# Holding back the first down-projection of each block, and tracking the residual in two column halves

## The chip, the cores and the metric

One core of one Trainium2 chip runs the whole program. The metric is the device time of one execution in microseconds (us); a kernel's figure is the median of its runs. A ratio is the mean time of one kernel's fast runs over the mean of the other's fast runs in the same rounds, so it is not quite the ratio of the medians; its 95% interval is in brackets.

## The reference, cut to what matters

Four layers run in turn on x of 2048 tokens x 576 columns: linear attention, bilinear unit, linear attention, bilinear unit. Each adds its result to x.

```python
def _B_ref(x, w_gate, w_up, w_down):          # F = 4608
    g = jnp.einsum("bsd,df->bsf", x, w_gate)
    u = jnp.einsum("bsd,df->bsf", x, w_up)
    h = g * u
    return jnp.einsum("bsf,fd->bsd", h, w_down)

x = x + _A_ref(_layernorm(x), A_wqkv, A_w_phi, A_wo)
x = x + _B_ref(_layernorm(x), B_w_gate, B_w_up, B_w_down)
# ... the same two lines once more
```

The change is in the bilinear unit.

## The kernel before

The kernel is written as coroutines, one for each piece of work. A scheduler, which runs when the kernel is built, asks each coroutine for its next group of instructions, estimates when that group could start, and takes the earliest. So every engine gets a **static order**. A tracker holds named keys (`("x", 5)` is row tile 5 of x) and places a semaphore wait wherever two instructions touch one key, and, for an accumulator bank in PSUM (`excl`), wherever two engines do.

The bilinear unit goes through 8 blocks of 256 tokens. A block has 36 rounds, one for each 128 columns of F. In a round TensorE does ten gate/up matmuls, ScalarE copies the gate half, VectorE multiplies (the product, `hT`), and TensorE does four down-projection matmuls, for the product of two rounds earlier (`LAG = 2`). These add up, over the block, in three banks: X and Y hold 512 columns of each half of the tokens, Z holds the remaining 64 columns of both. At the end of the block an epilogue of four VectorE adds moves the sums into x. There is only one set of X, Y, Z.

```python
        for i in range(total + LAG):
            if i < total:
                ...                                     # ten gate/up matmuls, copy, product
            if i >= LAG:
                b2, f2 = divmod(i - LAG, NF)            # NF = 36
                ...
                if f2 == 0 and b2 > 0:
                    yield ("wait", ("x2", L, b2 - 1))   # order: after the epilogue
                ...
                for sl in range(2):
                    bank = X if sl == 0 else Y
                    ...
                    ops.append(Op(d_pe(512), (... ps[:, bank, 0:512] ...), writes=[("acc", sl)], excl=[("pb", bank)]))
                    ops.append(Op(d_pe(64) + 6, (... ps[:, Z, 64 * sl:64 * sl + 64] ...), writes=[("accZ", sl)], excl=[("pb", Z)]))
                yield ("ops", "pe", ops)
                ...
                if f2 == NF - 1:
                    yield ("go", s.t_bepi(L, b2, on_block_done), 8, "bepi%d" % b2)
    ...
    def t_bepi(self, L, b, on_block_done):
        ...
        for sl in range(2):
            ...
            ops.append(Op(d_dve(512), (... tensor_tensor(xa, ps[:, bank, 0:512], xa, ALU.add)),
                          reads=[("acc", sl), ("x", st_)], writes=[("x", st_)], excl=[("pb", bank)]))
        for sl in range(2):
            ...
            ops.append(Op(d_dve(64), (... tensor_tensor(xb, ps[:, Z, 64 * sl:64 * sl + 64], xb, ALU.add)),
                          reads=[("accZ", sl), ("x", st_)], writes=[("x", st_)], excl=[("pb", Z)]))
```

While the first blocks of a bilinear unit run, the output half of the attention layer before it is still under way for later tokens. Its matmuls are mixed into the rounds of blocks 0 to 3 ("mixed stretch"). Blocks 4 to 7 are the "pure stretch".

Of the kernel before, what the change touches and what calls it, by code (L numbers as in the profile page):

```python
# [240 lines left out]
class Sched:  # L241
# [63 lines left out]
    def run(self):  # L305
        tr = self.tr
        while True:
# [50 lines left out]
            for th in self.threads:  # L358
                r = th.req
                if r[0] == "ops":  # L360
                    eng = r[1]
                    deps = []
                    for o in r[2]:
                        deps.extend(tr.deps_for(eng, o.reads, o.writes, o.excl))
                    est = max(self.free_at[eng], tr.ready_time(deps), th.t_ready)
                elif r[0] == "dma":
                    deps = tr.deps_for("sp", r[3], r[4], (), False)
                    est = max(self.free_at["sp"], tr.ready_time(deps), th.t_ready)
                else:
                    continue  # L370
                key = (est - self.bias.get(th.prio, 0.0), -th.prio)
                if best is None or key < best[0]:
                    best = (key, th, est)
            if best is None:
# [3 lines left out]
            _, th, est = best  # L378
# [42 lines left out]
CH = 3  # L421
# [3 lines left out]
def d_pe(n):  # L425
    return max(n, 64) / 2.4 + (7.0 if 288 <= n < 512 else 3.0)
# [18 lines left out]
class K:  # L445
    def __init__(self, nc, A_x, A_wqkv, A_w_phi, A_wo, B_w_gate, B_w_up, B_w_down, out, nlayers=4, dump=None):
        self.nc = nc
        self.A_x, self.A_wqkv, self.A_w_phi, self.A_wo = A_x, A_wqkv, A_w_phi, A_wo
        self.wg, self.wu, self.wd, self.out = B_w_gate, B_w_up, B_w_down, out
        self.nlayers = nlayers  # L450
        self.dump = dump
        self.nln0 = 3
        self.early = 2
        self.NPS, self.NSM, self.NVX, self.NET, self.NXP, self.NWD = 2, 4, 2, 3, 3, 3
        self.sbuf_check = True
        self.tr = Tracker()
        self.sc = Sched(self.tr)
        self.stack = ExitStack()
# [145 lines left out]
    def t_load(self):  # L604
# [10 lines left out]

        def xload(j):
            return grp("x%d" % j, [((lambda e: e.dma_start(s.x_sb[:, 4 * j:4 * j + 4, :], xv[:, 4 * j:4 * j + 4, :])),
                                    [("x", t) for t in range(4 * j, 4 * j + 4)], 128 * 4 * D * 2)], ("ld", "x", j))

        def rawload(which, kt):  # L620
            off = 0 if which == "q" else D
# [17 lines left out]
        for kt in range(5):  # L639
# [4 lines left out]
            ((lambda e: e.dma_start(s.Wvr[0:64, :], wqkv[512:576, 2 * D:2 * D + 324])), [("Wvr",)], 64 * 324 * 2),  # L644
            ((lambda e: e.dma_start(s.Wvr[64:128, 0:252], wqkv[512:576, 2 * D + 324:3 * D])), [("Wvr",)], 64 * 252 * 2),
        ], ("ld", "wv"))
        for j in range(1, 4):
            yield from xload(j)
        for kt in range(5):
            yield from rawload("q", kt)  # L650
        wov = s.A_wo[0:512, :].rearrange("(k p) n -> p k n", p=128)
        yield from grp("wo", [
            ((lambda e: e.dma_start(s.Wo[:], wov)), [("Wo",)], 512 * D * 2),
# [14 lines left out]
    def t_fuse(self, which):  # L668
# [2 lines left out]
        yield ("wait", "init")  # L671
        yield ("wait", "bdphi")
        if which == "q":
            yield ("wait", ("ain", 1, 1))
        yield ("go", s.t_fuse2(which), 6.6 if which == "q" else 8, "fuse2" + which)
        for kt in range(5):
            yield ("wait", ("ld", "raw", which, kt))
# [55 lines left out]
    def t_ln(self, b, sig):  # L733
# [6 lines left out]
        for j in range(2):  # L740
            for h in range(2):
                ops.append(Op(d_dve(288), (lambda e, j=j, h=h: e.bn_stats(st[:, sl[j], 6 * h:6 * h + 6], x_sb[:, ss[j], 288 * h:288 * h + 288])),
                              reads=[("x", ss[j])], writes=[("st", sl[j], h)]))
        yield ("ops", "dve", ops)
        ops = []
        for j in range(2):
# [15 lines left out]
        for j in range(2):  # L762
            ops.append(Op(800, (lambda e, j=j: e.tensor_scalar(  # L763
                xln[:, sl[j], 0:576], x_sb[:, ss[j], :], nm[:, sl[j]:sl[j] + 1], rstd[:, sl[j]:sl[j] + 1],
                ALU.add, ALU.mult)),
                reads=[("x", ss[j]), ("nmean", pair), ("rstd", pair), ("xlnpad",)], writes=[("xln", sl[j])]))
        yield ("ops", "pool", ops)
        for j in range(2):
            got = yield ("acq", ["pb", "pbx"])
# [107 lines left out]

    def t_ain(self, L, st_):
        s = self
        yield ("wait", ("w", "k"))  # L880
        ps_ = yield ("acq", "psb")
        sm = yield ("acq", "sm")
        yield ("go", s.t_v(L, st_), 6 + (NS - st_) / 100.0, "v%d_%d" % (L, st_))
        yield from s.softmax_front(st_, ps_, sm, s.Wk, s.Wkr, ("Wk",), ("Wkr",), ["pb", "pbx"])
        yield ("wait", ("v", L, st_))
        vxs = s.vx_of[(L, st_)]
# [33 lines left out]
    def t_aout(self, L, st_):  # L920
# [75 lines left out]
        for h in range(2):  # L996
# [3 lines left out]
            for k in range(5):  # L1000
# [3 lines left out]
                else:  # L1004
# [4 lines left out]
            yield ("ops", "pe", ops)  # L1009
            xs = s.x_sb[:, st_, 288 * h:288 * h + 288]  # L1010
            yield ("ops", "dve", [Op(d_dve(288), (lambda e, xs=xs, bank=bank: e.tensor_tensor(xs, s.ps[:, bank, 0:288], xs, ALU.add)),
                                     reads=[("pbd", bank), ("x", st_)], writes=[("x", st_)], excl=[("pb", bank)])])
            yield ("rel", got[0], got[1])
        yield ("rel", "et", et)
        yield ("sig", ("x1", L, st_))
# [16 lines left out]

    def t_bmain(self, L, on_block_done):
        s = self
        LAG = 2
        NG, NH = s.NG, s.NH
        ps, xT, Wg, Wu, Wr, gsb, hT = s.ps, s.xT, s.Wg, s.Wu, s.Wr, s.gsb, s.hT
        total = NB * NF
# [2 lines left out]
        yield ("wait", ("w", "q"))  # L1041
        yield ("wait", ("w", "k"))
        x0 = x1 = None
        X, Y, Z = s.ACC0, s.ACC0 + 1, s.ACC0 + 2
        for i in range(total + LAG):
            if i < total:
# [22 lines left out]
                if L == 1 and i < max(NG, NH):  # L1069
# [3 lines left out]
                yield ("ops", "dve", [Op(425, (lambda e, g=g, h=h, gub=gub: e.tensor_tensor(hT[:, h, :], ps[:, gub, 256:512], gsb[:, g, :], ALU.mult)),  # L1073
                                         reads=[("GUu", gub), ("gsb", g)], writes=[("hT", h)] + al, excl=[("pb", gub)])])
            if i >= LAG:
                b2, f2 = divmod(i - LAG, NF)
                h2 = (i - LAG) % NH
                c, fi = divmod(f2, CH)
                if f2 == 0 and b2 > 0:
                    yield ("wait", ("x2", L, b2 - 1))  # L1080
                if x0 is None:
                    gx = yield ("acqn", ["pbx"], 2)
                    x0, x1 = gx[0][1], gx[1][1]
                if fi == 0:
                    yield ("wait", ("wd", L, b2, c))
                slot = s.wd_slot[(L, b2, c)]
                ops = []
                for sl in range(2):
                    bank = X if sl == 0 else Y
                    lhsT = hT[:, h2, 128 * sl:128 * sl + 128]  # L1090
                    ops.append(Op(d_pe(512), (lambda e, lhsT=lhsT, bank=bank, slot=slot, fi=fi, f2=f2: e.matmul(  # L1091
                        ps[:, bank, 0:512], lhsT, s.wdr[:, slot, fi, 0:512], start=(f2 == 0), stop=(f2 == NF - 1))),
                        reads=[("hT", h2), ("wdr", slot)], writes=[("acc", sl)], excl=[("pb", bank)]))
                    ops.append(Op(d_pe(64) + 6, (lambda e, lhsT=lhsT, sl=sl, slot=slot, fi=fi, f2=f2: e.matmul(  # L1094
                        ps[:, Z, 64 * sl:64 * sl + 64], lhsT, s.wdr[:, slot, fi, 512:576],
                        start=(f2 == 0 and sl == 0), stop=(f2 == NF - 1), skip_group_check=True)),
                        reads=[("hT", h2), ("wdr", slot)], writes=[("accZ", sl)], excl=[("pb", Z)]))
                yield ("ops", "pe", ops)
                if fi == CH - 1:
                    yield ("rel", "wd", slot)  # L1100
                if f2 == NF - 1:
                    yield ("go", s.t_bepi(L, b2, on_block_done), 8, "bepi%d" % b2)
        yield ("wait", ("x2", L, NB - 1))
        yield ("rel", "pbx", x0)
        yield ("rel", "pbx", x1)
# [1 line left out]
    def t_bepi(self, L, b, on_block_done):  # L1107
        s = self
        ps, x_sb = s.ps, s.x_sb
        X, Y, Z = s.ACC0, s.ACC0 + 1, s.ACC0 + 2  # L1110
        ops = []
        for sl in range(2):
            st_ = 2 * b + sl
            bank = X if sl == 0 else Y
            xa = x_sb[:, st_, 0:512]
            ops.append(Op(d_dve(512), (lambda e, xa=xa, bank=bank: e.tensor_tensor(xa, ps[:, bank, 0:512], xa, ALU.add)),  # L1116
                          reads=[("acc", sl), ("x", st_)], writes=[("x", st_)], excl=[("pb", bank)]))
        for sl in range(2):
            st_ = 2 * b + sl
            xb = x_sb[:, st_, 512:576]  # L1120
            ops.append(Op(d_dve(64), (lambda e, xb=xb, sl=sl: e.tensor_tensor(xb, ps[:, Z, 64 * sl:64 * sl + 64], xb, ALU.add)),  # L1121
                          reads=[("accZ", sl), ("x", st_)], writes=[("x", st_)], excl=[("pb", Z)]))
        yield ("ops", "dve", ops)
        yield ("sig", ("x2", L, b))
        nxt = on_block_done(L, b)
        if nxt is not None:
            yield ("go", nxt, 6, "next%d_%d" % (L, b))

    def t_store(self, b):
        s = self  # L1130
        ov = s.out[0].rearrange("(t p) d -> p t d", p=128)
        yield ("dma", s.g_out, (lambda e: e.dma_start(ov[:, 2 * b:2 * b + 2, :], s.x_sb[:, 2 * b:2 * b + 2, :])),
               [("x", 2 * b), ("x", 2 * b + 1)], [("out", b)], 128 * 2 * D * 2, True)

    def t_layerA(self, L, first):
        s = self
# [47 lines left out]
    def build(self):  # L1184
        self.alloc()
        sc, tr, s = self.sc, self.tr, self
        self.g_out = tr.dma_group("out")
        sc.bias = {10: 300.0}
        sc.launch(self.t_init(), 9, "init")
        sc.launch(self.t_load(), 9, "load")  # L1190
        sc.launch(self.t_bdphi(), 9, "bdphi")
# [57 lines left out]
```

## Time and profile before

| | |
|---|---|
| time, median of the first 5 runs | 1257.26 us (1253.32 to 1259.26) |
| profiled span | 1254.8 us |
| attention input, layer 1 and layer 2 | about 0 to 130 us and 645 to 745 us |
| bilinear stretches | about 130 to 645 us and 745 to 1252 us |
| undisturbed round | 1.58 us |

The page of the kernel before: the span, the busy time of TensorE (PE) and its weight loads (PEld) with their shares of the span, the chain of work that ended last by engine and by line, and two groups of instructions (count, busy us, mean ns, idle before them and its releaser). L1058 and L1063 are the gate/up matmuls, L1091 and L1094 the down-projection of 512 and 64 columns.

```profile
span 1254.8 us, 25589 instructions
...
PE 1189.6 (95%) x10930; PEld 936.1 (75%) x11096; DVE 620.5 (49%) x1478; ACT 547.1 (44%) x1393; POOL 272.9 (22%) x268
...
PE 84%; DVE 5%; POOL 5%; ACT 4%; issue 1%; DMA 0%; SPq 0%; DVEq 0%
...
L1091 PE MATMUL ps<-wdr,hT 128*128 128x512 bf16 x986 | 318.8, 380 | 0.0
...
L1094 PE MATMUL ps<-wdr,hT 128*128 128x64 bf16 x1152 | 221.9, 193 | 14.8 <-DVE x_sb L1121 6.4
```

TensorE is the bound: 95% busy, 84% of the chain. The group of L1091 counts 986 matmuls where the group of L1094 has 1152; there are as many of one as of the other in the kernel, so 166 records are missing.

The view of waits of the same kernel (engine, tile, line, what it waited for: us in total, times, longest):

```profile
PEld ps L1094 <- DVE x_sb L1121: 6.4, 9, 0.8
PE ps L1094 <- DVE x_sb L1121: 6.4, 8, 0.8
```

TensorE waits 8 times for the last add of the epilogue (L1121). One such place in the timeline (start us, length us, engine, line, instruction; DVE is VectorE):

```profile
588.65 0.19 PE L1094 MATMUL ps<-wdr,hT 128*128 128x64 bf16 x1
...
588.68 0.60 PE L1058 MATMUL ps<-xT,Wg 128*128 128x256 bf16 x4
...
589.14 1.28 DVE L1116 TENSOR_TENSOR x_sb<-ps,x_sb 128x512 bf16<-128x512 f32 x2
...
589.66 0.27 PE L1063 MATMUL ps<-xT,Wr 128*128 128x256 bf16 x1
...
590.33 0.35 DVE L1121 TENSOR_TENSOR x_sb<-ps,x_sb 128x64 bf16<-128x64 f32 x2
...
590.74 0.20 PE L1094 MATMUL ps<-wdr,hT 128*128 128x64 bf16 x1 [0.80 <-DVE x_sb L1121]
...
590.77 0.38 PE L1091 MATMUL ps<-wdr,hT 128*128 128x512 bf16 x1
...
591.02 0.60 PE L1058 MATMUL ps<-xT,Wg 128*128 128x256 bf16 x4
```

The last matmul of the old block starts at 588.65. One gate/up group (588.68 to about 589.8) fills the time. VectorE begins the four adds at 589.14 (it had the product before them, from 588.80, to finish), and ends them at about 590.68. The 64-column matmul runs at 590.74, and the next gate/up group at 591.02. From 588.68 to 591.02 are 2.34 us, where an undisturbed round has 1.58: 0.76 us are lost. The round length is the safer measure here: the record of the 512-column matmul between is one of those missing, so "0.80" cannot be split into run and wait.

In the mixed stretch the same boundary loses nothing, because five attention matmuls (L799) lie in the gap:

```profile
818.58 0.60 PE L1058 MATMUL ps<-xT,Wg 128*128 128x256 bf16 x4
...
819.67 0.65 PE L799 MATMUL ps<-Wq,xT 128*128 128x288 bf16 x4
...
819.95 0.35 DVE L1121 TENSOR_TENSOR x_sb<-ps,x_sb 128x64 bf16<-128x64 f32 x2
...
820.28 0.38 PE L1091 MATMUL ps<-wdr,hT 128*128 128x512 bf16 x1
```

### The profile page before, as it was taken

Reading aid. Unit: us, or ns where it says so; the run is one execution under the profiler, and the core shown is the slowest. Engines: PE = TensorE matmul, PEld = TensorE weight load, DVE = VectorE, ACT = ScalarE, POOL = GpSimd, SP = SyncE. Lnnn points to the kernel's source line nnn. Section 1 sums busy time; section 2 is a strip of 40 time slices with the busy share of each in tenths; the row PEclk is TensorE's granted clock in tenths of the full one; section 3 lists DMA queues with packets and bytes.
Section 4 is the critical chain, followed back from the end, with each engine's and each line's share of the span. In section 5 each row is a group of like instructions: output and inputs, shape, how many; then the busy total and the mean of one; then the engine's idle time right before and its main releaser. Section 6 shows DMA issues by size and latency. Waiting matters only on the chain.

```text
span 1254.8 us, 25589 instructions
## 1 busy us (share of the span) xinstructions
PE 1189.6 (95%) x10930; PEld 936.1 (75%) x11096; DVE 620.5 (49%) x1478; ACT 547.1 (44%) x1393; POOL 272.9 (22%) x268
## 2 busy tenths in 40 slices
PE   6796999999999999999999889999999999999998
PEld 4574788788777777777767668777778777777776
DVE  6898646555553323323259975455545332323232
ACT  7887545345453222222248765444444322222222
POOL 4796212112120000000029842112112000000000
PEclk9998999999999999999999899999999999999999
DMA  9700122232222233333320002222323232333332
GB/s 312 231 2 1 29 79 80 72 87 72 77 82 86 86 99 87 97 89 87 98 72 2 1 1 72 83 84 76 91 72 96 72 109 86 109 88 108 90 105 67
DMA packets 85832, 104.61 MB, mean 83 GB/s; under 512 B 4374, under 2 KB 84566, under 8 KB 84566
## 3 DMA queue, kind: packets, MB, share of 16 engines
q1 hardware_dynamic: 85718, 102.96, 27.5%
q8 instruction: 87, 1.43, 0.4%
q14 instruction: 27, 0.22, 0.1%
HBM read 100.59 MB, written 2.36 MB: 82 GB/s over the span
## 4 chain that ended last, share of the span: by engine, by line
PE 84%; DVE 5%; POOL 5%; ACT 4%; issue 1%; DMA 0%; SPq 0%; DVEq 0%
PE ps L1058 25%; PE ps L1063 25%; PE ps L1091 17%; PE ps L1094 5%; PE ps L799 4%; PE ps L1007 3%; POOL dd L860 3%; PE ps L934 2%; POOL dd L824 1%; PE ps L953 1%; DVE ss L846 1%; PE ps L774 1%; DVE x_sb L1116 1%; PE ps L986 1%; DVE dd L832 1%
## 5 line engine op out<-in xcount | busy, mean ns | idle before, releaser
L1073 DVE TENSOR_TENSOR hT<-ps,gsb 128x256 bf16<-128x256 f32 x576 | 244.2, 424 | 580.4 <-ACT gsb L1071 578.8
L1071 ACT CAST gsb<-ps 128x256 bf16<-128x256 f32 x576 | 214.5, 372 | 626.2 <-PE ps L1063 588.3
L1058 PE MATMUL ps<-xT,Wg 128*128 128x256 bf16 x2304 | 347.3, 273 | 0.0
L1063 PE MATMUL ps<-xT,Wu 128*128 128x256 bf16 x2304 | 346.1, 273 | 0.0
L1091 PE MATMUL ps<-wdr,hT 128*128 128x512 bf16 x986 | 318.8, 380 | 0.0
L1058 PEld LDWEIGHTS ps<-xT,Wg 128*128 128x128 bf16 x2304 | 186.4, 98 | 82.1
L1063 PEld LDWEIGHTS ps<-xT,Wu 128*128 128x128 bf16 x2304 | 225.7, 98 | 26.3
L1094 PE MATMUL ps<-wdr,hT 128*128 128x64 bf16 x1152 | 221.9, 193 | 14.8 <-DVE x_sb L1121 6.4
L860 POOL TENSOR_TENSOR dd<-dd,rr 128x576 bf16<-128x576 bf16 x128 | 146.3, 1164 | 120.1 <-ACT rr L854 120.0
L1091 PEld LDWEIGHTS ps<-wdr,hT 128*128 128x128 bf16 x1152 | 112.5, 98 | 75.1 <-DVE x_sb L1116 1.7
L1058 PE MATMUL ps<-xT,Wr 128*128 128x256 bf16 x576 | 157.3, 273 | 0.0
L1063 PE MATMUL ps<-xT,Wr 128*128 128x256 bf16 x576 | 157.1, 273 | 0.0
L763 POOL TENSOR_SCALAR xln<-x_sb,nmean,rstd 128x576 bf16<-128x576 bf16 x64 | 52.1, 825 | 364.4 <-ACT rstd L758 364.4
L824 POOL TENSOR_TENSOR dd<-psb,mxmn 128x576 bf16<-128x576 bf16 x64 | 74.5, 1164 | 237.8 <-DVE mxmn L814 237.7
L1094 PEld LDWEIGHTS ps<-wdr,hT 128*128 128x128 bf16 x1152 | 112.3, 98 | 12.5 <-DVE x_sb L1121 6.4
L846 DVE TENSOR_REDUCE ss<-dd 128x64 f32<-128x1152 bf16 x64 | 86.4, 1351 | 22.4 <-ACT dd L841 22.1
L1058 PEld LDWEIGHTS ps<-xT,Wr 128*128 128x128 bf16 x576 | 56.5, 98 | 6.6
L1063 PEld LDWEIGHTS ps<-xT,Wr 128*128 128x128 bf16 x576 | 56.4, 98 | 6.6
L811 ACT CAST psb<-ps 128x288 bf16<-128x288 f32 x128 | 48.0, 401 | 17.8 <-PE ps L799 15.8
L937 ACT COPY eT<-ps 108x768 bf16<-108x768 bf16 x64 | 50.9, 799 | 8.3 <-PE ps L953 4.9
L819 DVE TENSOR_REDUCE mxmn<-ps 128x16 f32<-128x288 f32 x128 | 52.0, 448 | 0.0
L832 DVE TENSOR_TENSOR dd<-ps,mxmn 128x288 bf16<-128x288 f32 x128 | 51.8, 448 | 0.0
(85 smaller groups left out, 1142.6 us busy)
## 6 DMA issues: line engine op xcount, KB each, us to landing
wdr<-in_B_w_down_dram SPq DMA_DIRECT2D x192, 432.0 KB, 3.4
Wg<-in_B_w_gate_dram SPq DMA_DIRECT2D x4, 1152.0 KB, 13.0
Wu<-in_B_w_up_dram SPq DMA_DIRECT2D x4, 1152.0 KB, 28.5
x_sb<-in_A_x_dram SPq DMA_DIRECT2D x4, 576.0 KB, 6.2
out_dram<-x_sb SPq DMA_DIRECT2D x8, 288.0 KB, 3.4
Wraw<-in_A_wqkv_dram SPq DMA_DIRECT2D x8, 144.0 KB, 4.8
Wv<-in_A_wqkv_dram SPq DMA_DIRECT2D x1, 576.0 KB, 4.0
Wo<-in_A_wo_dram SPq DMA_DIRECT2D x1, 576.0 KB, 6.3
```

The source lines that it names most:

```text
L763: ops.append(Op(800, (lambda e, j=j: e.tensor_scalar(xln[:, sl[j], 0:576], x_sb[:, ss[j], :], nm[:, sl[j]:sl[j] + 1], rstd[:, sl[j]:sl[j] ...
L819: ops.append(Op(370, (lambda e, h=h, pv=pv: e.tensor_reduce(mxmn[:, pz, 1, 16 * h:16 * h + 16], pv, AX.X, ALU.min)), reads=[("pbd", bank)] ...
L824: yield ("ops", "pool", [Op(1170, (lambda e: e.tensor_tensor(d1, p3, mxb, ALU.subtract)), reads=[("psb", pz, 0), ("psb", pz, 1), ("mx", pz ...
L832: ops.append(Op(370, (lambda e, d2h=d2h, pv=pv, mnbh=mnbh: e.tensor_tensor(d2h, pv, mnbh, ALU.subtract)), reads=[("pbd", bank), ("mn", pz, ...
L846: Op(1320, (lambda e: e.tensor_reduce(ss[:, sm, :].rearrange("p (b g) -> p b g", b=2), e4, AX.X, ALU.add)), reads=s.ddk(sm, 0) + s.ddk(sm, ...
L860: yield ("ops", "pool", [Op(1150, (lambda e, ev=ev, rb=rb: e.tensor_tensor(ev, ev, rb, ALU.mult)), reads=s.ddk(sm, br) + [("rr", sm), ("dd ...
L1058: ops.append(Op(d_pe(256), (lambda e, lhsT=lhsT, rhs=rhs, k=k, gub=gub: e.matmul(ps[:, gub, 0:256], lhsT, rhs, start=(k == 0), stop=(k == ...
L1063: ops.append(Op(d_pe(256), (lambda e, lhsT=lhsT, rhs=rhs, k=k, gub=gub: e.matmul(ps[:, gub, 256:512], lhsT, rhs, start=(k == 0), stop=(k = ...
L1071: yield ("ops", "act", [Op(372, (lambda e, g=g, gub=gub: e.copy(gsb[:, g, :], ps[:, gub, 0:256])), reads=[("GUg", gub)], writes=[("gsb", g ...
L1073: yield ("ops", "dve", [Op(425, (lambda e, g=g, h=h, gub=gub: e.tensor_tensor(hT[:, h, :], ps[:, gub, 256:512], gsb[:, g, :], ALU.mult)), ...
L1091: ops.append(Op(d_pe(512), (lambda e, lhsT=lhsT, bank=bank, slot=slot, fi=fi, f2=f2: e.matmul(ps[:, bank, 0:512], lhsT, s.wdr[:, slot, fi, ...
L1094: ops.append(Op(d_pe(64) + 6, (lambda e, lhsT=lhsT, sl=sl, slot=slot, fi=fi, f2=f2: e.matmul(ps[:, Z, 64 * sl:64 * sl + 64], lhsT, s.wdr[: ...
```

## The change

The intent is to give the epilogue more time: at a block boundary the first down-projection of the new block is kept back until one more gate/up group has been issued, and then two down-projections go out together. So that the two 64-column adds can each follow their 512-column add without waiting for it to complete, the key of a row tile of x is split in two halves of columns. The diff, cut to its core:

```diff
+        pend = []
         for i in range(total + LAG):
             ...
             if i >= LAG:
+                pend.append(i - LAG)
                 b2, f2 = divmod(i - LAG, NF)
-                ... (the down-projection of round i - LAG)
+                if f2 == 0 and b2 > 0 and i + 1 < total:
+                    continue
+                for j in pend:
+                    ... (the down-projection of round j)
+                pend = []
@@ t_bepi
-                          reads=[("acc", sl), ("x", st_)], writes=[("x", st_)], excl=[("pb", bank)]))
-        for sl in range(2):
-            st_ = 2 * b + sl
+                          reads=[("acc", sl), ("x", st_, 0)], writes=[("x", st_, 0)], excl=[("pb", bank)]))
             xb = x_sb[:, st_, 512:576]
             ...
-                          reads=[("accZ", sl), ("x", st_)], writes=[("x", st_)], excl=[("pb", Z)]))
+                          reads=[("accZ", sl), ("x", st_, 1)], writes=[("x", st_, 1)], excl=[("pb", Z)]))
```

All other users of x name both halves. The diff also turns some constants into attributes with the same values (`lag`, `bias`, and flags that are off), and the scheduler looks up its bias by the whole part of a priority.

More of the change, by code (lines that the diff above doesn't have):

```diff
@@ L370, in run @@
                     continue
-                key = (est - self.bias.get(th.prio, 0.0), -th.prio)
+                key = (est - self.bias.get(int(th.prio), 0.0), -th.prio)
                 if best is None or key < best[0]:
@@ L455, in __init__ @@
         self.sbuf_check = True
+        self.lag = 2
+        self.bias = {10: 300.0}
+        self.qfuse_after = ("ain", 1, 1)
+        self.rawq_early = False
+        self.v_early = False
         self.tr = Tracker()
@@ L617, in xload @@
             return grp("x%d" % j, [((lambda e: e.dma_start(s.x_sb[:, 4 * j:4 * j + 4, :], xv[:, 4 * j:4 * j + 4, :])),
-                                    [("x", t) for t in range(4 * j, 4 * j + 4)], 128 * 4 * D * 2)], ("ld", "x", j))
+                                    [("x", t, c_) for t in range(4 * j, 4 * j + 4) for c_ in range(2)], 128 * 4 * D * 2)], ("ld", "x", j))
         def rawload(which, kt):
@@ L646, in t_load @@
         ], ("ld", "wv"))
+        if s.rawq_early:
+            for kt in range(5):
+                yield from rawload("q", kt)
         for j in range(1, 4):
             yield from xload(j)
-        for kt in range(5):
-            yield from rawload("q", kt)
+        if not s.rawq_early:
+            for kt in range(5):
+                yield from rawload("q", kt)
         wov = s.A_wo[0:512, :].rearrange("(k p) n -> p k n", p=128)
@@ L673, in t_fuse @@
         if which == "q":
-            yield ("wait", ("ain", 1, 1))
+            yield ("wait", s.qfuse_after)
         yield ("go", s.t_fuse2(which), 6.6 if which == "q" else 8, "fuse2" + which)
@@ L742, in t_ln @@
                 ops.append(Op(d_dve(288), (lambda e, j=j, h=h: e.bn_stats(st[:, sl[j], 6 * h:6 * h + 6], x_sb[:, ss[j], 288 * h:288 * h + 288])),
-                              reads=[("x", ss[j])], writes=[("st", sl[j], h)]))
+                              reads=[("x", ss[j], 0), ("x", ss[j], 1)], writes=[("st", sl[j], h)]))
         yield ("ops", "dve", ops)
@@ L765, in t_ln @@
                 ALU.add, ALU.mult)),
-                reads=[("x", ss[j]), ("nmean", pair), ("rstd", pair), ("xlnpad",)], writes=[("xln", sl[j])]))
+                reads=[("x", ss[j], 0), ("x", ss[j], 1), ("nmean", pair), ("rstd", pair), ("xlnpad",)], writes=[("xln", sl[j])]))
         yield ("ops", "pool", ops)
@@ L879, in t_ain @@
         s = self
+        if s.v_early:
+            yield ("go", s.t_v(L, st_), 6 + (NS - st_) / 100.0, "v%d_%d" % (L, st_))
         yield ("wait", ("w", "k"))
@@ L882, in t_ain @@
         sm = yield ("acq", "sm")
-        yield ("go", s.t_v(L, st_), 6 + (NS - st_) / 100.0, "v%d_%d" % (L, st_))
+        if not s.v_early:
+            yield ("go", s.t_v(L, st_), 6 + (NS - st_) / 100.0, "v%d_%d" % (L, st_))
         yield from s.softmax_front(st_, ps_, sm, s.Wk, s.Wkr, ("Wk",), ("Wkr",), ["pb", "pbx"])
@@ L1011, in t_aout @@
             yield ("ops", "dve", [Op(d_dve(288), (lambda e, xs=xs, bank=bank: e.tensor_tensor(xs, s.ps[:, bank, 0:288], xs, ALU.add)),
-                                     reads=[("pbd", bank), ("x", st_)], writes=[("x", st_)], excl=[("pb", bank)])])
+                                     reads=[("pbd", bank), ("x", st_, 0), ("x", st_, 1)], writes=[("x", st_, 0), ("x", st_, 1)], excl=[("pb", bank)])])
             yield ("rel", got[0], got[1])
@@ L1034, in t_bmain @@
         s = self
-        LAG = 2
+        LAG = s.lag
         NG, NH = s.NG, s.NH
@@ L1075, in t_bmain @@
             if i >= LAG:
+                pend.append(i - LAG)
                 b2, f2 = divmod(i - LAG, NF)
-                h2 = (i - LAG) % NH
-                c, fi = divmod(f2, CH)
-                if f2 == 0 and b2 > 0:
-                    yield ("wait", ("x2", L, b2 - 1))
-                if x0 is None:
-                    gx = yield ("acqn", ["pbx"], 2)
-                    x0, x1 = gx[0][1], gx[1][1]
-                if fi == 0:
-                    yield ("wait", ("wd", L, b2, c))
-                slot = s.wd_slot[(L, b2, c)]
@@ L1087, in t_bmain @@
-                ops = []
-                for sl in range(2):
-                    bank = X if sl == 0 else Y
-                    lhsT = hT[:, h2, 128 * sl:128 * sl + 128]
-                    ops.append(Op(d_pe(512), (lambda e, lhsT=lhsT, bank=bank, slot=slot, fi=fi, f2=f2: e.matmul(
-                        ps[:, bank, 0:512], lhsT, s.wdr[:, slot, fi, 0:512], start=(f2 == 0), stop=(f2 == NF - 1))),
-                        reads=[("hT", h2), ("wdr", slot)], writes=[("acc", sl)], excl=[("pb", bank)]))
-                    ops.append(Op(d_pe(64) + 6, (lambda e, lhsT=lhsT, sl=sl, slot=slot, fi=fi, f2=f2: e.matmul(
-                        ps[:, Z, 64 * sl:64 * sl + 64], lhsT, s.wdr[:, slot, fi, 512:576],
-                        start=(f2 == 0 and sl == 0), stop=(f2 == NF - 1), skip_group_check=True)),
-                        reads=[("hT", h2), ("wdr", slot)], writes=[("accZ", sl)], excl=[("pb", Z)]))
@@ L1098, in t_bmain @@
-                yield ("ops", "pe", ops)
-                if fi == CH - 1:
-                    yield ("rel", "wd", slot)
-                if f2 == NF - 1:
-                    yield ("go", s.t_bepi(L, b2, on_block_done), 8, "bepi%d" % b2)
+                if f2 == 0 and b2 > 0 and i + 1 < total:
+                    continue
+                for j in pend:
+                    b2, f2 = divmod(j, NF)
+                    h2 = j % NH
+                    c, fi = divmod(f2, CH)
+                    if f2 == 0 and b2 > 0:
+                        yield ("wait", ("x2", L, b2 - 1))
+                    if x0 is None:
+                        gx = yield ("acqn", ["pbx"], 2)
+                        x0, x1 = gx[0][1], gx[1][1]
+                    if fi == 0:
+                        yield ("wait", ("wd", L, b2, c))
+                    slot = s.wd_slot[(L, b2, c)]
+                    ops = []
+                    for sl in range(2):
+                        bank = X if sl == 0 else Y
+                        lhsT = hT[:, h2, 128 * sl:128 * sl + 128]
+                        ops.append(Op(d_pe(512), (lambda e, lhsT=lhsT, bank=bank, slot=slot, fi=fi, f2=f2: e.matmul(
+                            ps[:, bank, 0:512], lhsT, s.wdr[:, slot, fi, 0:512], start=(f2 == 0), stop=(f2 == NF - 1))),
+                            reads=[("hT", h2), ("wdr", slot)], writes=[("acc", sl)], excl=[("pb", bank)]))
+                        ops.append(Op(d_pe(64) + 6, (lambda e, lhsT=lhsT, sl=sl, slot=slot, fi=fi, f2=f2: e.matmul(
+                            ps[:, Z, 64 * sl:64 * sl + 64], lhsT, s.wdr[:, slot, fi, 512:576],
+                            start=(f2 == 0 and sl == 0), stop=(f2 == NF - 1), skip_group_check=True)),
+                            reads=[("hT", h2), ("wdr", slot)], writes=[("accZ", sl)], excl=[("pb", Z)]))
+                    yield ("ops", "pe", ops)
+                    if fi == CH - 1:
+                        yield ("rel", "wd", slot)
+                    if f2 == NF - 1:
+                        yield ("go", s.t_bepi(L, b2, on_block_done), 8, "bepi%d" % b2)
@@ L1116, in t_bepi @@
             ops.append(Op(d_dve(512), (lambda e, xa=xa, bank=bank: e.tensor_tensor(xa, ps[:, bank, 0:512], xa, ALU.add)),
-                          reads=[("acc", sl), ("x", st_)], writes=[("x", st_)], excl=[("pb", bank)]))
-        for sl in range(2):
-            st_ = 2 * b + sl
+                          reads=[("acc", sl), ("x", st_, 0)], writes=[("x", st_, 0)], excl=[("pb", bank)]))
             xb = x_sb[:, st_, 512:576]
             ops.append(Op(d_dve(64), (lambda e, xb=xb, sl=sl: e.tensor_tensor(xb, ps[:, Z, 64 * sl:64 * sl + 64], xb, ALU.add)),
-                          reads=[("accZ", sl), ("x", st_)], writes=[("x", st_)], excl=[("pb", Z)]))
+                          reads=[("accZ", sl), ("x", st_, 1)], writes=[("x", st_, 1)], excl=[("pb", Z)]))
         yield ("ops", "dve", ops)
@@ L1132, in t_store @@
         yield ("dma", s.g_out, (lambda e: e.dma_start(ov[:, 2 * b:2 * b + 2, :], s.x_sb[:, 2 * b:2 * b + 2, :])),
-               [("x", 2 * b), ("x", 2 * b + 1)], [("out", b)], 128 * 2 * D * 2, True)
+               [("x", 2 * b, 0), ("x", 2 * b, 1), ("x", 2 * b + 1, 0), ("x", 2 * b + 1, 1)], [("out", b)], 128 * 2 * D * 2, True)
     def t_layerA(self, L, first):
@@ L1187, in build @@
         self.g_out = tr.dma_group("out")
-        sc.bias = {10: 300.0}
+        sc.bias = dict(self.bias)
         sc.launch(self.t_init(), 9, "init")
```

## The prediction

> **What bounds the kernel.** TensorE: the page gives it 1189.6 us busy of a 1254.8 us span (95%), and the chain of work that ended last is 84% TensorE. Two stretches (about 0 to 130 us and 645 to 745 us, attention input) are held by VectorE and GpSimd; the change does not touch those. In the two bilinear stretches one round (ten gate/up matmuls, then four down-projection matmuls) repeats every 1.58 us in the timeline (501.95 to 503.53), back to back.
>
> **The target.** At the end of each of 8 blocks per layer, four VectorE adds fold the accumulators into x. The first down-projection of the next block writes the same three banks, so it waits. In the timeline at 588.7 us: the old block's last down-projection ends about 588.8; the adds start at 589.14, after the product of the round before, and end about 590.68 (two of 681 ns, two of 215 ns, overlapping: 1.55 us); TensorE has only one gate/up group (1.09 us) to fill with, and its 64-column matmul starts at 590.74. That round took 2.34 us (588.68 to 591.02): 0.76 us too long. The Trainium skill, "PSUM — Partial Sum Buffer", section "Engine vs sequencer instructions", says that matmuls start and complete in program order and that VectorE's queue is strict FIFO. The trace agrees: the next gate/up group does not pass the blocked matmul.
>
> The view of waits lists this wait 8 times, 6.4 us in all. They are the boundaries at 414, 472, 530, 589, 1022, 1080, 1138 and 1195 us; the same eight show in the chain as VectorE adds of 1.28 us. The other six (209, 279, 349, 819, 889, 959 us) already have attention-output projections or transposes in the gap and lose at most 0.1 us.
>
> **What the change does.** It holds back a block's first down-projection by one round, so two gate/up groups (2.17 us) stand before it, then issues two together. No matmul, byte or VectorE operation is added or removed. TensorE then reaches the accumulators about 590.9, after the adds' release at 590.74: the wait goes, with a margin near 0.15 us. The ring of four hT buffers just suffices; the product of the held-back round must finish before its gate/up bank is written again: about 592.9 against 593.4, even when the four normalization statistics (1.53 us) go before it. Splitting the residual's key lets each 64-column add stand behind its 512-column add without waiting for it to complete; the four still take about 1.55 us. The other changed lines keep their old values.
>
> **Sum.** 8 x 0.76 = 6.1 us, all on the critical path as TensorE is the bound there. Against it: the static order in the mixed stretches is recomputed and may shift a microsecond either way. Expected 1257.3 - 6.1 = 1251.2 us (0.5%). Range 1246.5 to 1255.5, since runs of before alone spread 1253.3 to 1259.3. Chances: faster by over 2% 0.02, within 2% 0.97, slower 0.01.
>
> **What would show it.** Right: the down-projection's waits on the x adds (6.4 us) fall under 1 us; blocks in the pure stretch take 57.5 us instead of 58.25 in layer 1 (414.37 to 472.63) and 56.9 instead of 57.7 in layer 2; TensorE busy stays 1189 to 1190 us; the eight adds leave the chain; attention input phases keep their length. Wrong: a remaining wait of some tenths per boundary (margin too thin), a new TensorE wait on VectorE's product two rounds later, or a changed length in the mixed or attention phases from reordering. A gain well over 8 us would mean that the six covered boundaries also lost time, or that the reordering helped.

## The result, and the profile after

| | before | after |
|---|---|---|
| median | 1258.08 us (16 runs) | 1252.06 us (9 runs) |
| ratio | | 0.9955 [0.9943, 0.9967] |
| profiled span | 1254.8 us | 1252.0 us |

The result is 0.45% less time, and clear of noise. The page after; here L1109 and L1112 are the down-projection, L1071 and L1076 the gate/up matmuls, L1135 and L1138 the adds:

```profile
span 1252.0 us, 25573 instructions
...
PE 1192.3 (95%) x10930; PEld 938.3 (75%) x11096; DVE 619.6 (49%) x1478; ACT 547.1 (44%) x1393; POOL 272.9 (22%) x268
...
L1109 PE MATMUL ps<-wdr,hT 128*128 128x512 bf16 x986 | 316.9, 380 | 0.4 <-DVE x_sb L1135 0.4
...
L1112 PE MATMUL ps<-wdr,hT 128*128 128x64 bf16 x1152 | 221.9, 193 | 9.4 <-DVE x_sb L1138 0.5
```

The groups of the down-projection now show next to no idle time that the adds ended. The view of waits of TensorE from 745 us on has what is left; from 210.8 to 643 us there is none:

```profile
PE ps L1112 <- DVE x_sb L1138: 0.5, 1, 0.5
PE ps L1109 <- DVE x_sb L1135: 0.4, 1, 0.4
```

A pure boundary after the change, in the timeline:

```profile
530.79 0.19 PE L1112 MATMUL ps<-wdr,hT 128*128 128x64 bf16 x1
...
530.82 0.60 PE L1071 MATMUL ps<-xT,Wg 128*128 128x256 bf16 x4
...
531.27 0.68 DVE L1135 TENSOR_TENSOR x_sb<-ps,x_sb 128x512 bf16<-128x512 f32 x1
...
531.87 0.21 DVE L1138 TENSOR_TENSOR x_sb<-ps,x_sb 128x64 bf16<-128x64 f32 x1
531.91 0.60 PE L1071 MATMUL ps<-xT,Wg 128*128 128x256 bf16 x4
...
532.60 0.21 DVE L1138 TENSOR_TENSOR x_sb<-ps,x_sb 128x64 bf16<-128x64 f32 x1
...
532.89 0.27 PE L1076 MATMUL ps<-xT,Wr 128*128 128x256 bf16 x1
...
533.22 0.19 PE L1112 MATMUL ps<-wdr,hT 128*128 128x64 bf16 x1
```

Two gate/up groups (530.82 and 531.91) now lie between the two blocks. The adds end at about 532.81; the 64-column matmul comes at 533.22 with no wait before it. (The 512-column matmul before it has no record; by its width it starts 0.22 us earlier.) One whole block of the pure stretch, from its first add to the next block's, in the view of windows (us, then busy us and count of PE, PEld, DVE, ACT, POOL, then the granted clock, DMA share and GB/s), before and after:

```profile
472.63:530.88 58.25, 57.03 (x508) 44.78 (x515) 18.29 (x47) 15.65 (x43) 1.63 (x2) 1.00 0.32 92
```

```profile
473.78:531.27 57.49, 57.02 (x508) 44.88 (x515) 18.18 (x47) 15.55 (x43) 1.63 (x2) 1.00 0.32 94
```

TensorE is busy for the same 57.0 us and the block is 0.76 us shorter. (508 matmul records stand here against 515 weight loads. In after_again, the changed kernel profiled once more with no record missing, TensorE is busy for 57.50 of the 57.50 us of this block.) The page "TensorE: Matmul & The Clock Gate" of the Trainium skill (section "Wait — 56ns, not 53.3ns?") gives a warm matmul of N columns N / 2.4 GHz + about 2.5 ns from start to start. By this estimate the matmuls of this block, counted from the static order, make 57.50 us, which is what the trace has after the change: 57.49. With these matmuls at this rate TensorE has nothing left to gain there. (An undisturbed round has 3712 columns in 14 matmuls: 1.58 us by this sum and by the trace.)

**An account of all rounds.** The same sum can be set against every round: take the time between the first gate matmuls of two neighbouring rounds, and subtract what the matmuls between them (known from the static order) take at full speed. What remains is an estimate of the time that TensorE lost in that round; missing records do no harm. Losses by block, in us, from the traces:

```
                 layer 1, blocks 0..7                      layer 2, blocks 0..7
before           4.11 .03 .03 .17 .76 .76 .76 .76          2.47 .03  .03  .02 .76 .76 .76 .76
after            4.07 .18 .02 .17 .00 .00 .00 .00          2.44 .35 1.59  .02 .00 .00 .00 .00
```

So the change gains 8 x 0.76 = 6.1 us, and gives back 0.15 us in layer 1 and 1.9 us in layer 2. (What block 0 loses is the passage from the attention stretch; it varies from run to run with the clock, as the last section shows, and the change does not reach it.) The largest piece given back, 1.25 us, is at the boundary near 890 us:

```profile
887.97 0.19 PE L1112 MATMUL ps<-wdr,hT 128*128 128x64 bf16 x1
...
888.14 0.75 DVE L823 TENSOR_REDUCE mxmn<-psb 128x32 f32<-128x576 bf16 x1 [0.22 <-ACT psb L820]
...
888.81 0.81 DVE L828 TENSOR_REDUCE mxmn<-ps 128x16 f32<-128x288 f32 x2
...
890.04 0.68 DVE L1135 TENSOR_TENSOR x_sb<-ps,x_sb 128x512 bf16<-128x512 f32 x1
890.07 0.27 PE L1076 MATMUL ps<-xT,Wr 128*128 128x256 bf16 x1
...
890.77 0.39 PE L1109 MATMUL ps<-wdr,hT 128*128 128x512 bf16 x1 [0.43 <-DVE x_sb L1135]
...
891.64 0.20 PE L1112 MATMUL ps<-wdr,hT 128*128 128x64 bf16 x1 [0.47 <-DVE x_sb L1138]
```

The last matmul of the old block starts at 887.97, but VectorE first has three reductions of the attention output to do (888.14 and 888.81) and then the product (at 889.70), so the adds begin only at 890.04 instead of some 0.3 us after the block's end. Even two gate/up groups do not cover that. In the kernel before, attention matmuls lay in this gap and the reductions came after the adds. The smaller pieces are not at boundaries: in the two rounds that lose 0.32 us (at 826.67 and 896.18) five transposes of the attention output (L998) start at 828.07 and 897.58, just after the VectorE multiplication that makes their input (L987) ends (828.02 and 897.53).

Two profiles are no measure of a gain of this size: the spans differ by 2.8 us, the medians by 6. The first epilogue, up to which both kernels have one and the same TensorE order, came at 209.05 us in one and at 210.80 us in the other.

### The profile page after: what moved, and what is told of

The parts are those of the page before. It is cut to its first block, busy times and chain, and to the rows that moved or that the text cites. A ratio compares the mean times of both kernels' runs of the same rounds, so it can differ in the third digit from the quotient of the medians.

```text
span 1252.0 us, 25573 instructions
## 1 busy us (share of the span) xinstructions
PE 1192.3 (95%) x10930; PEld 938.3 (75%) x11096; DVE 619.6 (49%) x1478; ACT 547.1 (44%) x1393; POOL 272.9 (22%) x268
## 4 chain that ended last, share of the span: by engine, by line
PE 84%; DVE 8%; ACT 4%; POOL 2%; issue 1%; DMA 0%; SPq 0%; DVEq 0%
PE ps L1071 25%; PE ps L1076 25%; PE ps L1109 17%; PE ps L1112 5%; PE ps L808 4%; PE ps L1019 3%; DVE ss L855 3%; PE ps L946 2%; POOL dd L869 1%; PE ps L965 1%; DVE dd L841 1%; PE ps L783 1%; DVE mxmn L823 1%; DVE mxmn L828 1%; PE ps L998 1%
## 5 line engine op out<-in xcount | busy, mean ns | idle before, releaser
L1071 PE MATMUL ps<-xT,Wg 128*128 128x256 bf16 x2304 | 347.3, 273 | 0.0
L1076 PE MATMUL ps<-xT,Wu 128*128 128x256 bf16 x2304 | 346.1, 273 | 0.0
L1109 PE MATMUL ps<-wdr,hT 128*128 128x512 bf16 x986 | 316.9, 380 | 0.4 <-DVE x_sb L1135 0.4
L1071 PEld LDWEIGHTS ps<-xT,Wg 128*128 128x128 bf16 x2304 | 187.3, 98 | 80.8
L1076 PEld LDWEIGHTS ps<-xT,Wu 128*128 128x128 bf16 x2304 | 225.7, 98 | 26.4
L1112 PE MATMUL ps<-wdr,hT 128*128 128x64 bf16 x1152 | 221.9, 193 | 9.4 <-DVE x_sb L1138 0.5
L1109 PEld LDWEIGHTS ps<-wdr,hT 128*128 128x128 bf16 x1152 | 112.5, 98 | 76.8 <-DVE x_sb L1135 0.7
L1071 PE MATMUL ps<-xT,Wr 128*128 128x256 bf16 x576 | 157.2, 273 | 0.0
L1076 PE MATMUL ps<-xT,Wr 128*128 128x256 bf16 x576 | 157.2, 273 | 0.0
L1112 PEld LDWEIGHTS ps<-wdr,hT 128*128 128x128 bf16 x1152 | 112.7, 98 | 6.5 <-DVE x_sb L1138 0.8
L1071 PEld LDWEIGHTS ps<-xT,Wr 128*128 128x128 bf16 x576 | 56.5, 98 | 6.6
L1076 PEld LDWEIGHTS ps<-xT,Wr 128*128 128x128 bf16 x576 | 56.4, 98 | 6.6
```

Of the source, the lines that this page charges most:

```text
L1071: ops.append(Op(d_pe(256), (lambda e, lhsT=lhsT, rhs=rhs, k=k, gub=gub: e.matmul(ps[:, gub, 0:256], lhsT, rhs, start=(k == 0), stop=(k == ...
L1076: ops.append(Op(d_pe(256), (lambda e, lhsT=lhsT, rhs=rhs, k=k, gub=gub: e.matmul(ps[:, gub, 256:512], lhsT, rhs, start=(k == 0), stop=(k = ...
L1109: ops.append(Op(d_pe(512), (lambda e, lhsT=lhsT, bank=bank, slot=slot, fi=fi, f2=f2: e.matmul(ps[:, bank, 0:512], lhsT, s.wdr[:, slot, fi, ...
L1112: ops.append(Op(d_pe(64) + 6, (lambda e, lhsT=lhsT, sl=sl, slot=slot, fi=fi, f2=f2: e.matmul(ps[:, Z, 64 * sl:64 * sl + 64], lhsT, s.wdr[: ...
```

## The experiments

Theory: the gain is the longer TensorE work between the last down-projection of a block and the first of the next, at the eight pure boundaries. Rivals: the split key shortens the adds; the reordering of the mixed stretches gives part of the gain; the later reading of the product is what helps.

| kernel | median | before, same rounds | ratio |
|---|---|---|---|
| split_only | 1258.55 | 1257.76 | 1.0004 [0.9991, 1.0016] |
| hold_only | 1252.24 | 1257.76 | 0.9956 [0.9943, 0.9968] |
| hold_early | 1259.85 | 1257.76 | 1.0016 [1.0000, 1.0031] |
| hold_late | 1250.85 | 1257.76 | 0.9943 [0.9929, 0.9957] |
| lag3 | 1255.22 | 1258.54 | 0.9979 [0.9947, 1.0010] |
| before_longer | 1277.72 | 1258.54 | 1.0150 [1.0112, 1.0187] |
| after_longer | 1259.24 | 1258.54 | 1.0008 [0.9984, 1.0032] |
| one_key | 1252.28 | 1258.54 | 0.9955 [0.9926, 0.9984] |
| after_again | 1252.36 | 1256.75 | 0.9967 [0.9951, 0.9983] |
| hold_late_again | 1250.25 | 1256.75 | 0.9948 [0.9930, 0.9965] |

All gave correct results.

### One part alone: the split key, or the hold-back

split_only, from the kernel after:

```diff
-                if f2 == 0 and b2 > 0 and i + 1 < total:
-                    continue
```

> The changed kernel with the hold-back switched off: only the split key and the new order of the four adds remain; its TensorE order equals that of before. Theory (the held-back down-projection gives the gain): the eight waits of about 0.8 us stay (6 to 7 us in the view of waits), time within 0.15% of before. Rival (the split key shortens the adds and thereby the wait): some of the 6 us gain appears here, waits fall below 5 us.

Measured: ratio 1.0004, and the wait is all there. View of waits of TensorE in split_only:

```profile
PE ps L1110 <- DVE x_sb L1136: 6.4, 8, 0.8
```

Its TensorE order is that of before, instruction for instruction, which also shows that the attributes of the diff do nothing. The split alone is worth nothing.

hold_only, from the kernel after:

```diff
-   reads=[("acc", sl), ("x", st_, 0)], writes=[("x", st_, 0)]
+   reads=[("acc", sl), ("x", st_, 0), ("x", st_, 1)], writes=[("x", st_, 0), ("x", st_, 1)]
+        for sl in range(2):          # the 64-column adds after both 512-column adds, as before
+            st_ = 2 * b + sl
     ... (the 64-column add with both keys, too)
```

> The hold-back with the old order of the adds and every add tied to both halves of x; its TensorE order equals that of the changed kernel. Theory: the whole gain, about 5.5 to 6 us (0.45%), the eight waits gone, the one new wait near 890 us (0.9 us) still there. Rival (the split is needed): waits of some tenths remain at each boundary and the gain is under 4 us.

Measured: ratio 0.9956, the same as the whole change; no loss at the pure boundaries, and 1.25 us lost in the round near 890 us. The hold-back is the whole gain.

### The hold-back at some boundaries only

hold_early and hold_late, from the kernel after:

```diff
-                if f2 == 0 and b2 > 0 and i + 1 < total:
+                if f2 == 0 and 1 <= b2 <= 3 and i + 1 < total:     # hold_early
+                if f2 == 0 and b2 >= 4 and i + 1 < total:          # hold_late
```

> Hold-back only at the three first boundaries of each layer, which were already covered by attention-output matmuls. Theory: no gain; the eight waits of 0.8 us stay and the new one of 0.9 us near 890 us is added: time from equal to before to 1 us longer. Rival (covered boundaries also lost time): 1 to 3 us faster than before.

Measured: 1.0016, which is 2.0 us longer than before (the interval just reaches no change), twice the 1 us that was expected at most. View of waits of hold_early:

```profile
PE ps L1112 <- DVE x_sb L1138: 4.9, 9, 0.8
...
PE ps L1109 <- DVE x_sb L1135: 0.4, 1, 0.4
```

These lines name 0.5 + 0.4 us of new wait (the other entries of L1112 are the eight old boundaries, which the account still puts at 0.76 us each; why a list of waits can show less is told under lag3). The account of rounds finds more: 1.25 us at the boundary near 890, 0.32 us in each of two other rounds of layer 2, and 0.15 us in layer 1, together 2.05 us. That is the measured loss.

> Hold-back only at the last four boundaries of each layer, where TensorE had nothing to fill the gap. Theory: 8 x 0.76 = 6.1 us less than before, no wait on the adds in the profile at all, also none near 890 us; so equal to or up to 1 us better than the changed kernel. Rival (reordering of the mixed stretches gave part of the gain): clearly less than the changed kernel, by over 1 us.

Measured: 0.9943, and 0.9948 when repeated. No TensorE wait on the adds is left in the trace, and the account has 0.00 at the pure boundaries and 0.02 to 0.03 us in blocks 1 and 2 (0.16 in block 3 of layer 1, as before). By the account this version beats both kernels, the change by 2.0 us where at most 1 us was expected. So the reordering of the mixed stretches does not give part of the gain; by the account it takes back a third of it.

To set the two side by side, both were run again on one chip.

> The changed kernel unaltered, to set it beside the late hold-back on one chip. Accounting of gaps between gate/up groups says 8 x 0.76 us gained and about 2.0 us given back by the reordered mixed stretches: 4 us (0.32%) less than before.

> Hold-back at the last four boundaries of each layer, once more. The same accounting says 6.1 us (0.48%) less than before, thus 2.0 us less than the changed kernel.

Measured: 0.33% and 0.52% less than before, where the account had said 0.32% and 0.48%; medians 2.1 us apart. The intervals of the two overlap, so the 2 us rest on the account as much as on the timing. For the change, the first measurement had 5.7 us (0.45%) and the account has 4.0; whether the difference is more than noise stays open.

### A later reading of the product

lag3, from the kernel before:

```diff
-        LAG = 2
+        LAG = 3
```

> The kernel before with every down-projection three rounds behind its gate/up group in place of two; there is still one gate/up group between the last down-projection of a block and the first of the next. Theory (what counts is the TensorE work between those two): the eight waits of 0.8 us stay, time within 0.3% of before. Rival (what counts is the time from the VectorE product to the down-projection that reads it): the waits go and 4 us or more are gained.

Measured: 0.9979 [0.9947, 1.0010], which the timing leaves unclear. The trace is clearer: each of the eight boundaries still loses 0.76 us by the account. The expectation that the waits would again be listed as 0.8 us each missed: the view shows eight of 0.5 us. View of waits of lag3, then the timeline, which has the reason:

```profile
PE ps L1094 <- DVE x_sb L1121: 3.8, 8, 0.5
```

```profile
530.44 0.27 PE L1063 MATMUL ps<-xT,Wr 128*128 128x256 bf16 x1
530.65 0.39 PE L1091 MATMUL ps<-wdr,hT 128*128 128x512 bf16 x1
...
531.51 0.20 PE L1094 MATMUL ps<-wdr,hT 128*128 128x64 bf16 x1 [0.47 <-DVE x_sb L1121]
```

Here the 512-column matmul has its record, at 530.65, so that the view counts only the wait after it. The loss is unchanged. The rival falls, since one round more between product and use did not remove any of it.

### A longer epilogue

before_longer and after_longer, the same edit in both kernels, ahead of the four adds (with the keys of the memory that the spare buffer shares):

```diff
+        ops.append(Op(d_dve(512), (lambda e: e.tensor_copy(s.scr[:], ps[:, X, 0:512])),
+                      reads=[("acc", 0)], writes=[("scr",)] + al, excl=[("pb", X)]))
```

> The kernel before with one more VectorE operation ahead of the four adds, a copy of the first 512-column accumulator to a spare buffer, about 0.60 us as the adds are spaced. Theory: there is no slack at the eight boundaries, each loses 0.60 us more (1.36 us in all), and the six covered ones, with about 0.15 us of slack, lose up to 0.45 us each: 5 to 7.5 us longer than before.

> The changed kernel with the same extra copy. Theory, with the slack of 0.35 us that the trace of the changed kernel shows (64-column matmul at 533.22, adds over at 532.81): each of the eight boundaries waits 0.25 us, about 2 us in all, plus 0.6 us at the boundary near 890: 2 to 3 us longer than the changed kernel. With the slack of 0.15 us that the prediction named: 0.45 us each, 3.6 us in all. Rival (the gain came from something other than the slack): the copy costs as much as in the kernel before.

Measured at the pure boundaries, by the account: 1.35 to 1.36 us in before_longer (0.76 before, so the whole 0.60 is added) and 0.26 us in after_longer. Both are as expected: there was no slack before, and there are 0.60 - 0.26 = 0.34 us of slack after.

The total times missed, by far: 19 us longer instead of 5 to 7.5, and some 6.7 us longer than the kernel after (0.53%) instead of 2 to 3. By the account, most of what was not expected goes with the static order, which the scheduler made anew. In the attention input of layer 2 the two kernels have the same TensorE order as each other, differing in 80 of 716 places from that of before and after, and this stretch took 4.3 us longer in before_longer and 3.3 us in after_longer (0.6 of it the copy in the last epilogue of layer 1). The ten other profiles, all with one TensorE order there, lie within 1.5 us of each other. That the order is the cause is argued from this; no run has the new order without the copy. In before_longer, two boundaries of the mixed stretch lost about 4.6 us each, the pattern of 890 us again, with reductions ahead of the copy and the adds. One of the two, in the timeline:

```profile
898.59 0.81 DVE L821 TENSOR_REDUCE mxmn<-ps 128x16 f32<-128x288 f32 x2
...
899.81 0.68 DVE L1117 CAST scr<-ps 128x512 bf16<-128x512 f32 x1
900.41 1.28 DVE L1123 TENSOR_TENSOR x_sb<-ps,x_sb 128x512 bf16<-128x512 f32 x2
...
901.15 0.39 PE L1093 MATMUL ps<-wdr,hT 128*128 128x512 bf16 x1 [2.12 <-DVE x_sb L1123]
```

### One key

one_key, from the kernel after: the order of adds of the change, each with both keys of its row tile.

> The changed kernel with the new order of the adds but one key for each row of x, so each 64-column add waits for its 512-column add to complete. Theory: the four adds take 0.1 to 0.3 us longer, which the slack of 0.35 us takes up; no wait at the eight boundaries, time within 0.15% of the changed kernel. Rival (the split key is needed for the gain): waits of 0.1 us and more at each.

Measured: 0.9955, no loss at the pure boundaries. The adds at one of them:

```profile
527.94 0.68 DVE L1135 TENSOR_TENSOR x_sb<-ps,x_sb 128x512 bf16<-128x512 f32 x1
...
528.66 0.23 DVE L1138 TENSOR_TENSOR x_sb<-ps,x_sb 128x64 bf16<-128x64 f32 x1
...
528.80 0.68 DVE L1135 TENSOR_TENSOR x_sb<-ps,x_sb 128x512 bf16<-128x512 f32 x1
```

From a 512-column add to the 64-column add after it are 0.72 us here (527.94 to 528.66), and 0.60 us with split keys (531.27 to 531.87, shown above). So the split saves about 0.12 us on each of two adds, which the slack hides. It showed only where slack was missing: the boundary near 890 lost 1.50 us instead of 1.25. (The scheduler also made another order for part of layer 1's mixed stretch; from there on the TensorE orders of one_key and of the change are the same.)

## Why the prediction was right or wrong

- **Total.** 1251.2 us predicted, 1252.06 measured, inside the range. Right; but that it came so close is in part luck. The account has 6.1 us gained and 2.0 given back, and the repeat measured about 4 us (0.33%), not the 6.0 by which the medians of the first measurement differ.
- **The eight waits of 0.76 us.** Right as to place, size and cause: the pure blocks went from 58.25 to 57.49 us (57.5 predicted) in layer 1 and from 57.70 to 56.94 us (56.9 predicted) in layer 2. hold_only and hold_late show the cause, before_longer that TensorE had no slack.
- **Program order.** The prediction drew on the Trainium skill, "PSUM — Partial Sum Buffer", section "Engine vs sequencer instructions". The traces agreed: no gate/up group passed a blocked down-projection (in before_longer TensorE stood for 2.12 us near 899 us), and the adds kept their place behind the product or the reductions.
- **The six covered boundaries.** Right: hold_early gained nothing there. (One of them, at 349 us, loses 0.15 us in the kernel before, where at most 0.1 was predicted.)
- **A static order that "may shift a microsecond either way".** This is the step that was off. The hold-back at covered boundaries moved attention matmuls and with them VectorE's reductions, and cost 2.0 us, 1.25 of it at one boundary. A changed length of the mixed stretches was one of the prediction's own signs of being wrong, and it came. Only the pure boundary had been worked through; the covered ones were taken as safe because they had lost nothing.
- **A margin near 0.15 us.** It is 0.34 us by after_longer. The term was mis-sized because the release of the adds was set against the 512-column matmul, which does not need the last add; the 64-column one does, and comes 0.22 us later.
- **The split key.** Rightly taken as not worth time by itself.
- **TensorE busy 1189 to 1190 us.** Wrong: 1192.3. The surplus arose before any instruction was moved: up to the first epilogue the busy time is 176.5 us before and 179.1 us after (view of windows), in one and the same TensorE order.
- **The adds leave the chain.** Right: after the change, of the adds only the one at the very end (1247.67 us) is among the long pieces of the chain.

## What to carry to other kernels

Where an accumulator is single-buffered, compare the length of its evacuation with the work that stands between its last and its next write; if the work is too short, a larger distance at that one place can close the gap (here to 0.00 us at eight boundaries). Do it only where the gap is empty: where other work covers it, moving instructions in a static order can make a new stall, and a rebuilt order can cost more than the edit itself. To judge gains of a few us in 1250, take repeated times, and account rounds of the trace against full-speed work instead of comparing two spans or two lists of waits.

## What the Trainium skill lacked or had wrong

- "VectorE: DVE Perf Modes", section "The DRAIN you can't avoid", says of its chained copies that "the semaphore costs nothing extra here". A wait of a VectorE add on the VectorE add before it cost 0.12 us (0.72 against 0.60 us from start to start, 512 columns out of PSUM).
- "TensorE: Matmul & The Clock Gate", Part 1, calls the clock gate's window free-running and a kernel's warm-up variable from run to run. The runs agree that it varies and add how large this is late in a kernel: in the same order up to the first epilogue, that epilogue began between 206.8 and 211.8 us in nine profiles (that the clock alone makes this spread is not shown). At the change to layer 2's bilinear stretch, the first round lost 0.26 to 0.30 us in six profiles and 1.63 us in four, all with one TensorE order before it. This goes with the granted clock there: from 730 to 740 us it was 0.83 in the six and 0.66 or 0.67 in the four. The view of windows of before (0.30 us lost; columns as above, the clock is the first number after POOL) and of split_only (1.63 us lost):

```profile
730.00:740.00 10.00, 7.11 (x59) 5.28 (x57) 7.48 (x21) 7.60 (x20) 5.04 (x6) 0.83 0.00 1
```

```profile
730.00:740.00 10.00, 6.93 (x41) 4.51 (x40) 6.39 (x18) 6.69 (x18) 4.99 (x5) 0.66 0.00 1
```

- The same page, section "Wait — 56ns, not 53.3ns?", measured N / 2.4 GHz + 2.5 ns for one width at a time. It held here for blocks that mix 64, 256 and 512 columns with a weight load for each matmul: 57.50 us summed, 57.49 us in the trace.
- The pages on notification queues tell of lost records in general; none says that a trace can lack records of one kind of matmul alone, at the same places in several profiles. In six profiles here 166 of the 1152 records of the 512-column matmul were missing, in the six others none (after and after_again are one kernel), and one and the same loss of 0.76 us was listed as a wait of 0.80 us where the record was missing and of 0.47 us where it was there.
